# The outermost dimension of a transfer: loads and stores of the last rows of x and w1 with rows outermost, in place of 2 or 4 groups

## The chip, the cores and the metric

One core of one Trainium2 chip. The time is device microseconds of one execution of the whole program; lower is better. A profiled execution gives the trace from which the views below are taken.

## The reference

x has 2048 rows of 576 numbers. All is float32.

```python
xn = layernorm(x)
s  = linear_attention(xn, wqkv) @ wo          # 32 heads of 18, phi(t) = where(t>0, t+1, exp(t)) + 1e-6
h  = gelu(xn @ w1 + b1)                       # w1 [576, 4608]
g  = silu(h @ w2 + b2)                        # w2 [4608, 576]
out = x + s * g
```

The attention has no softmax over rows: per head it is (phi(q) (phi(k)^T v)) / (phi(q) z), with z the sum of phi(k) over the rows.

## The kernel before

**Precision.** Each matrix operand is kept as a high part (float32r) and the rest that the high part leaves out, and a product is high x high + high x rest + rest x high. ScalarE (ACT) makes the high part, VectorE (DVE) subtracts it to get the rest (`set_hi`, `set_lo`, L649 to L653).

**First stage.** For each of 16 tiles of 128 rows of x (loop at L431): load (`load_x`, three tiles ahead), layernorm on DVE with a power on GpSimd (POOL), transposes on TensorE (PE, tile `pt`), then the projections to k (`pk`) and v (`pv`) at L226 and the state phi(k)^T v. Beside it the loop prepares weights for later: it loads w2 (`w2_load`), makes sums of its blocks, splits them and stores them as operands (`w2_store`, L313); and it does the same for the last 64 rows of w1 (`we_load` L326, `we_sums` L331 on POOL, `we_hi`, `we_lo`, `we_store` L346). There are five groups q of the latter; each leaves a tile `w1h` of 128 rows with a high and a low part of 7 x 128 columns side by side, and `we_store` writes each part to `we_dram`.

**Second stage.** The same for q: project, normalize, transpose, and `attend` (`ps_s`, L626), which multiplies with kv already folded into wo and stores s to `s_dram`. Beside it the class `XSums` makes the sums of blocks of x that the main loop needs, and the class `Rest` (L758) does that for the last 64 of the 576 columns: `gather` and `whole` collect them, `split` makes high and low parts and writes them with four stores to `rq_dram` (L795).

**Main loop.** x @ w1 and h @ w2 are each done on 2 x 2 blocks with seven products in place of eight. The 2048 rows are two halves, and each half goes through nine chunks of four column tiles of w1: 18 steps. A step does 14 up products (`Up.step`, PE line L959, tiles `a`, `b`, `zy`, `e`; seven matmuls each) and then seven down products (`product`, PE line L1089, tile `pm`, 168 matmuls), added into `macc`. The 512 first rows of w1 come in through `W1` in the first half (raw, L679; the operands are made on chip and stored, L647) and through `W1Loaded` in the second half (L733, L740). The last 64 rows of w1 come through `load_we` (L662, DMA at L666), twice a step: a tile `we` of 128 partitions, in which partitions 0 to 63 and 64 to 127 hold the same 64 rows (32 rows of high part, 32 of low part). The seventh matmul of each product uses it against the matching tile of x, whose 128 rows are loaded by `load_rest` (L807): the high part twice and the low part twice, 32 rows each. In the second half a step also loads all seven operands of w2 (L1029), and for one tile of the first half's rows the finished sum, s and x (`finish_load`, L1178 to L1180, tiles `fin`); POOL combines them (`finish`, L1184, L1185) and stores the output (L1186). Between the halves seven tiles of x of 1 MB are loaded (`load_x_part`, L1252). The last step has no blocks to sum: it uses w2 as it is (`down_plain`, tile `pd`, L1209) and writes the last outputs.

**What sets the order.** PE, ACT, DVE and POOL follow an order written out in the code: each action of a step has a place (`add(base + n, ...)`, run by `at_step` after each product). All DMAs are issued by SyncE (SP) in one list, in order; an issue first waits for the tile or the DRAM tensor it touches, and for one of eight DMA semaphores, which are used in turn: so at most eight transfers are under way, and the issue after them waits until the one eight before it has landed.

The layouts around the change, each followed by the access it is used with:

```python
    rq_dram = dram.tile([2, 8, P, 512], F32, name="rq_dram")              # L117
    we_dram = dram.tile([4 * WG, 2, 32, WB * P], F32, name="we_dram")     # L118
        d = we_dram.rearrange("(g q) v r c -> q v g r c", q=WG)           # L344: store of 4 groups x 32 rows
            bass.AP(tensor=src.tensor, offset=src.offset, ap=[[0, 2], [WB * P, 64], [1, WB * P]]),  # L668
```

## Time and profile before

| | |
|---|---|
| time, median of 3 runs | 1250.49 us (1247.34 to 1253.26) |
| the profiled execution's own time | 1250.95 us |
| its span, first to last instruction | 1249.2 us |
| mean granted PE clock | 0.953 |
| DMA queue of SyncE | 85135 packets, 264.94 MB, 62.4% of 16 engines' span |
| HBM | 166.69 MB read, 96.27 MB written |

The span is cut into instructions per engine; "busy" is the union of their times. A window is a stretch of the span, with the busy time of each engine in it, the clock that PE was granted (1.00 is full), the mean busy share of the core's 16 DMA engines, and the rate in GB/s. A line of 40 digits cuts a window (or the span) in 40 slices; a digit is the busy share in tenths. The chain is followed back from the last instruction to what released each step; a row has its start, its length and what it was, "DMA a<-b" being a transfer from its issue to its landing, and "SPq" SyncE's own list. A row on waits says who waited for whom, the total, how often, and the longest. A row on issues has duration ns min/median/max of the issuing instruction and its first and last start.

### The profile page before, as it was taken

Reading aid. Unit: us, or ns where it says so; the run is one execution under the profiler, and the core shown is the slowest. Engines: PE = TensorE matmul, PEld = TensorE weight load, DVE = VectorE, ACT = ScalarE, POOL = GpSimd, SP = SyncE. Lnnn points to the kernel's source line nnn. Section 1 sums busy time; section 2 is a strip of 40 time slices with the busy share of each in tenths; the row PEclk is TensorE's granted clock in tenths of the full one; section 3 lists DMA queues with packets and bytes.
Section 4 is the critical chain, followed back from the end, with each engine's and each line's share of the span. In section 5 each row is a group of like instructions: output and inputs, shape, how many; then the busy total and the mean of one; then the engine's idle time right before and its main releaser. Section 6 shows DMA issues by size and latency. Waiting matters only on the chain.

```text
span 1249.2 us, 18534 instructions
## 1 busy us (share of the span) xinstructions
PE 1136.9 (91%) x6972; PEld 1044.1 (84%) x6972; DVE 816.6 (65%) x1159; ACT 456.7 (37%) x771; POOL 448.4 (36%) x392
## 2 busy tenths in 40 slices
PE   8965799999889899999999995989989989989888
PEld 8865798999779789989989984878787977978868
DVE  6733465989656778878877874547365563654657
ACT  4422353334342543544444352314123232232333
POOL 4634463433234534533553451304134042240430
PEclk9987899999989999999999997989989999999889
DMA  7655653256576495586567587876676566766542
GB/s 282 219 218 188 262 213 119 80 188 238 170 286 228 169 330 215 198 297 252 201 256 281 206 255 260 287 236 178 199 232 196 176 189 189 217 201 186 180 157 87
DMA packets 85224, 266.12 MB, mean 213 GB/s; under 512 B 8973, under 2 KB 19469, under 8 KB 81551
## 3 DMA queue, kind: packets, MB, share of 16 engines
q1 hardware_dynamic: 85135, 264.94, 62.4%
q8 instruction: 55, 0.90, 0.3%
q14 instruction: 34, 0.28, 0.1%
HBM read 166.69 MB, written 96.27 MB: 210 GB/s over the span
## 4 chain that ended last, share of the span: by engine, by line
PE 59%; DMA 27%; DVE 4%; SPq 3%; POOL 2%; issue 2%; ACT 1%; POOLq 0%; DVEq 0%; ACTq 0%
PE pm L1089 24%; PE e L959 6%; PE zy L959 6%; PE a L959 5%; DMA w1u<-w1e 3%; PE pv L226 3%; PE pq L226 3%; PE b L959 3%; DMA fin4h<-x 3%; PE pk L226 3%; PE ps_s L626 2%; DMA we<-op 2%; DMA we_dram<-w1h 2%; DMA fin2h<-x 2%; PE pd L1209 2%
## 5 line engine op out<-in xcount | busy, mean ns | idle before, releaser
L1096 DVE TENSOR_TENSOR macc<-pm,macc 128x576 f32<-128x576 f32 x218 | 164.4, 754 | 68.1 <-PE pm L1089 66.5
L650 ACT CAST h_h<-g 128x512 fp32r<-128x512 f32 x204 | 121.5, 620 | 174.0 <-PE pm L1089 138.2
L653 DVE TENSOR_TENSOR h_l<-g,h_h 128x512 fp32r<-128x512 f32 x204 | 168.1, 829 | 6.9 <-ACT h_h L650 6.6
L1184 POOL TENSOR_TENSOR fin1l<-fin1h,fin1l 128x288 f32<-128x288 f32 x8 | 6.5, 818 | 258.0 <-DMA fin1l<-s_dram 155.6
L1058 POOL TENSOR_TENSOR mid<-g 128x512 f32<-128x512 f32 x34 | 44.6, 1312 | 104.1 <-ACT g L967 104.1
L1052 POOL TENSOR_TENSOR g<-g 128x512 f32<-128x512 f32 x34 | 53.0, 1559 | 38.5 <-DVE h_l L653 36.6
L967 ACT ACTIVATE g<-b,b1c 128x512 f32<-128x512 f32 x36 | 24.8, 689 | 114.6 <-DVE b L985 114.6
L976 ACT COPY mid<-a 128x512 f32<-128x512 f32 x36 | 21.1, 587 | 123.8 <-PE a L959 123.8
L979 DVE TENSOR_TENSOR mid<-b,mid 128x512 f32<-128x512 f32 x36 | 24.7, 687 | 61.1 <-PE b L959 59.4
L694 POOL TENSOR_TENSOR w1raw<-w1raw 128x256 f32<-128x256 f32 x18 | 16.9, 937 | 130.6 <-DVE wa L710 130.6
L653 DVE TENSOR_TENSOR h_l<-mid,h_h 128x512 fp32r<-128x512 f32 x34 | 44.9, 1321 | 21.7 <-ACT h_h L650 21.0
L959 PE MATMUL a<-xh,wa 128*128 128x512 f32 x144 | 51.7, 399 | 6.9 <-ACT g L967 3.8
L1055 POOL TENSOR_TENSOR g<-g 128x512 f32<-128x512 f32 x34 | 54.5, 1604 | 2.7
L959 PE MATMUL a<-h0r,wa 128*128 128x512 f32 x144 | 50.6, 392 | 0.0
L982 DVE TENSOR_TENSOR mid<-zy,mid 128x512 f32<-128x512 f32 x36 | 24.9, 691 | 37.3 <-PE zy L959 37.2
L203 PE MATMUL pt<-ident,xn 128*128 128x128 f32 x80 | 13.5, 306 | 38.3 <-ACT xn L198 37.0
L1049 POOL TENSOR_TENSOR g<-g 128x512 f32<-128x512 f32 x34 | 46.4, 1364 | 2.7
L985 DVE TENSOR_TENSOR b<-e,mid 128x512 f32<-128x512 f32 x36 | 25.2, 699 | 31.7 <-PE e L959 31.6
L959 PE MATMUL b<-s2r,we 128*128 128x512 f32 x126 | 34.7, 418 | 12.0 <-issue 7.7
L591 POOL TENSOR_TENSOR pbuf<-phiq,den 128x576 f32<-128x576 f32 x16 | 20.0, 1251 | 66.7 <-DVE den L590 52.1
L203 PEld LDWEIGHTS pt<-ident,xn 128*128 128x128 f32 x80 | 10.2, 155 | 40.4 <-ACT xn L198 38.6
L295 POOL TENSOR_TENSOR w2r<-w2r 128x576 f32<-128x576 f32 x27 | 41.5, 1543 | 0.7
(810 smaller groups left out, 3700.0 us busy)
## 6 DMA issues: line engine op xcount, KB each, us to landing
we<-we_dram SPq DMA_DIRECT2D x36, 448.0 KB
op<-w2o SPq DMA_DIRECT2D x27, 576.0 KB
w2raw<-w SPq DMA_DIRECT2D x10, 1152.0 KB
w2r<-w SPq DMA_DIRECT2D x9, 1152.0 KB
w1raw<-w SPq DMA_DIRECT2D x18, 512.0 KB
op_a<-wa SPq DMA_DIRECT2D x18, 512.0 KB
op_c<-wc SPq DMA_DIRECT2D x18, 512.0 KB
op_d<-wd SPq DMA_DIRECT2D x18, 512.0 KB
```

Of the source, the lines that this page charges most:

```text
L226: nc.tensor.matmul(ps[:, h, :HD], st, w[:, k, h * HD : (h + 1) * HD], start=(i == 0), stop=(i == len(seq) - 1),)
L295: nc.gpsimd.tensor_tensor(dst, a, b, op=SUB)
L650: nc.scalar.copy(pair[0], src)
L653: eng.tensor_tensor(pair[1], src, pair[0].bitcast(F32), op=SUB)
L959: nc.tensor.matmul(ps, st, mv, start=first and n == 0, stop=n == len(seq) - 1, skip_group_check=True,)
L985: tt(B, E, u2_sb, op=ADD)
L1049: tt(src[5, pr], A(1, 0), A(1, 1), op=ADD)
L1052: tt(src[6, pr], src[5, pr], A(0, 0), op=SUB)
L1055: tt(src[3, pr], A(0, 1), src[6, pr], op=SUB)
L1058: tt(src[7, pr], A(0, 0), A(1, 0), op=SUB)
L1089: nc.tensor.matmul(ps[:, q, :HD], hs[p][st][:, cs], m[:, p, :], start=(n == 0 and i not in CHAIN), stop=(n == len(seq) - 1), skip_group_ch ...
L1096: nc.vector.tensor_tensor(dst, src, dst, op=ADD)
```

## The change

Three tensors or accesses take another shape. `rq_dram` and `we_dram` now hold the rows in DRAM in the order in which they stand on chip, row by row, with the high and the low part of a row side by side. A store therefore has the 128 partitions as its outermost dimension on both sides: one store per group in `we_store` (high and low part together, 896 KB) in place of two with four groups outermost; two stores in `Rest.split` in place of four. A load of `we` becomes two loads of 64 rows, one for each half of the partitions, in place of one load whose source has an outermost dimension of 2 with step 0. A load of a rest becomes two loads of 64 partitions, each with 32 source rows outermost and each row repeated twice inside.

```diff
-    rq_dram = dram.tile([2, 8, P, 512], F32, name="rq_dram")
-    we_dram = dram.tile([4 * WG, 2, 32, WB * P], F32, name="we_dram")
+    rq_dram = dram.tile([2, 2, P, 2, 512], F32, name="rq_dram")
+    we_dram = dram.tile([WG, P, 2, WB * P], F32, name="we_dram")
...
     def we_store(q):
-        d = we_dram.rearrange("(g q) v r c -> q v g r c", q=WG)
-        for v in range(2):
-            nc.sync.dma_start(d[q, v], we_op(q, v).bitcast(F32))
+        src = we["h", q % 2][:, : 2 * WB * P].bitcast(F32)
+        nc.sync.dma_start(we_dram[q].rearrange("p v c -> p (v c)"), src)
...
     def load_we(n):
 
         we_sb[n] = w1p.tile([P, WB, P], F32R, tag="we", name=f"we_{n}", bufs=2)
-        src = we_dram[n % NP]
-        nc.sync.dma_start(
-            we_sb[n].bitcast(F32).rearrange("p b c -> p (b c)"),
-            bass.AP(tensor=src.tensor, offset=src.offset, ap=[[0, 2], [WB * P, 64], [1, WB * P]]),
-        )
+        dst = we_sb[n].bitcast(F32).rearrange("p b c -> p (b c)")
+        g, q = divmod(n % NP, WG)
+        src = we_dram[q, 32 * g : 32 * g + 32].rearrange("r v c -> (r v) c")
+        for k in range(2):
+            nc.sync.dma_start(dst[64 * k : 64 * k + 64], src)
...
         def split(self, k):
             src = (self.q, self.e)[k]
-            h, l = self.two(f"s{k}")
+            h, l = t = self.two(f"s{k}")
             nc.scalar.copy(h, src)
             nc.vector.tensor_tensor(l, src, h.bitcast(F32), op=SUB)
-            for n, v in enumerate((h, h, l, l)):
-                nc.sync.dma_start(
-                    rq_dram[self.half, 4 * k : 4 * k + 4, 32 * n : 32 * n + 32], v.bitcast(F32)
-                )
+            for v in range(2):
+                nc.sync.dma_start(rq_dram[self.half, k, :, v], t[v].bitcast(F32))
...
     def load_rest(half, i, dst):
 
-        nc.sync.dma_start(dst.bitcast(F32), rq_dram[half, REST_AT[i]])
+        k, at = divmod(REST_AT[i], 4)
+        for v in range(2):
+            src = rq_dram[half, k, 32 * at : 32 * at + 32, v]
+            nc.sync.dma_start(
+                dst[64 * v : 64 * v + 64].bitcast(F32),
+                bass.AP(tensor=src.tensor, offset=src.offset, ap=[[1024, 32], [0, 2], [1, 512]]),
+            )
```

## The prediction

> **What bounds the kernel now.** I read the page first, then the chain of work that ended last, a table of windows by stage, and the windows in which TensorE (PE) waits.

> ```profile
> span 1249.2 us, 18534 instructions
> ...
> PE 1136.9 (91%) x6972; PEld 1044.1 (84%) x6972; DVE 816.6 (65%) x1159; ACT 456.7 (37%) x771; POOL 448.4 (36%) x392
> ...
> PE 59%; DMA 27%; DVE 4%; SPq 3%; POOL 2%; issue 2%; ACT 1%; POOLq 0%; DVEq 0%; ACTq 0%
> ```

> PE does nearly all the work, yet over a quarter of the chain is transfers. The windows show where (columns: busy us of each engine with its instructions, granted PE clock, busy share of the 16 DMA engines, GB/s):

> ```profile
> 32.67:140.05 107.38, 70.33 (x499) 68.75 (x498) 50.63 (x85) 34.73 (x57) 45.59 (x52) 0.83 0.61 219
> 140.05:194.50 54.45, 54.45 (x422) 54.45 (x423) 37.02 (x63) 25.13 (x42) 29.54 (x23) 0.99 0.59 220
> 202.00:336.30 134.30, 132.98 (x986) 128.58 (x985) 109.44 (x165) 51.80 (x96) 45.86 (x36) 1.00 0.47 151
> 336.30:445.60 109.30, 96.55 (x534) 85.45 (x533) 69.74 (x98) 42.74 (x74) 40.52 (x34) 0.94 0.65 235
> 445.60:760.60 315.00, 315.00 (x1864) 285.68 (x1863) 255.14 (x348) 143.13 (x250) 139.19 (x116) 1.00 0.69 245
> 760.60:880.50 119.90, 97.84 (x535) 85.66 (x534) 62.42 (x80) 33.90 (x52) 30.16 (x22) 0.89 0.75 245
> 880.50:1187.90 307.40, 283.48 (x1597) 256.11 (x1597) 170.36 (x228) 88.42 (x144) 87.80 (x72) 0.95 0.63 195
> 1187.90:1249.20 61.30, 50.05 (x292) 44.95 (x290) 39.16 (x50) 20.01 (x32) 12.10 (x7) 0.93 0.35 122
> ```

> From 336.30 on these are steps of the main loop: 0 and 1; 2 to 8; 9 and 10; 11 to 16; 17. Steps 2 to 8 take 315.00 / 7 = **45.0 us** each with PE busy throughout and its clock at 1.00: that is the floor of a step, and a PE that never rests isn't throttled here. The other steps lose time, and so does the first stage. There, the chain gives one row per value projection (pv) of a tile of x:

> ```profile
> 14.19 3.84 PE pv L226 x28
> ...
> 23.61 3.77 PE pv L226 x28
> ...
> 32.67 3.77 PE pv L226 x28
> ...
> 48.73 40.46 DMA w1u<-w1e x2
> 89.25 25.18 DMA we_dram<-w1h
> ...
> 140.05 4.44 PE pv L226 x28
> ...
> 194.50 3.77 PE pv L226 x28
> ...
> 329.56 14.05 DMA xh<-rq_dram
> ...
> 738.83 12.73 SPq L740
> ...
> 788.07 1.61 PE a L959 x7
> ...
> 804.76 27.71 DMA we<-op
> ...
> 928.85 18.28 DMA fin4h<-x
> ...
> 1198.36 2.27 DMA fin3l<-s_dram
> ...
> 1218.25 22.42 PE pd L1209 x168
> ```

> Of sixteen tiles the rows at 14.19, 23.61 and 32.67 are the first three and 194.50 is the last. At the pace of the undisturbed rows (9.1 us) 140.05 is the tenth: the last six tiles took (194.50 - 140.05) / 6 = 9.08 us each. The seven tiles between 32.67 and 140.05 should take 63.5 us and took 107.4: **43.9 us lost**, and the chain there is a load of w1e and a store to we_dram. Note also that small transfers with nothing ahead of them land in 2.27 us, others after 14 to 28 us.

> Why so late? One step (13, 984.0 to 1035.4) in 40 slices of 1.285 us, and a wait of the first stage:

> ```profile
> DMA  9997311259857920301689999999811111697999
> GB/s 259 322 254 207 113 50 53 72 154 262 309 161 164 373 98 26 121 0 56 136 328 379 402 393 268 263 257 257 243 67 50 49 50 51 144 350 249 267 277 271
> ```

> ```profile
> 95.00:101.00 6.00, 0.00 (x0) 0.00 (x0) 0.00 (x0) 0.00 (x0) 0.00 (x0) 0.50 0.24 84
> ```

> A row of ones at 50 GB/s is two engines of sixteen (2/16 = 0.125), 25 GB/s each; 0.24 is four of sixteen. Everything on PE is idle at 95 to 101, and four engines still carry data. The program has two kinds of transfer with such a count outermost: the load of we (outermost dimension the two repeats) and the stores to we_dram and rq_dram (outermost dimension 4).

> ```profile
> we<-we_dram SPq DMA_DIRECT2D x36, 448.0 KB
> we_dram<-w1h SPq DMA_DIRECT2D x10, 448.0 KB
> rq_dram<-wa_rest0s SPq DMA_DIRECT2D x8, 256.0 KB
> ```

> So **two (or four) engines are the bound, not all sixteen.** Step 13 moves 195 GB/s x 51.4 us = 10.0 MB. Without its two loads of we (0.92 MB) an engine has 9.1/16 = 0.57 MB; at the rate of a busy engine there (195 / 0.63 / 16 = 19.3 GB/s) 29.5 us. The two engines have 2 x 448 KB / 2 / 25 GB/s = 18.3 us more: 47.8 us, above the 45.0 of PE. All later transfers have a share on those two engines and land behind it.

> **The change, part by part.** (1) The load of we becomes two loads of 64 rows; an engine gets 1/16 of both: 2.3 us a step in place of 18.3 on two. (2) Ten stores of 448 KB on four engines (10 x 448 KB / 4 / 25 GB/s = 46 us on each of the four) become five of 896 KB over 128 rows, 11.5 us on each engine. (3) Sixteen stores to rq_dram become eight over 128 rows. They lie in 202.00:336.30, where PE is busy 132.98 of 134.30 us: nothing to gain. (4) Fourteen loads of rests become 28 of 64 rows, with 32 outermost in the source. The order of instructions on PE, DVE, ACT and POOL is the same in both programs; only SyncE's list changes, by 36 + 14 - 5 - 8 = 37 more issues.

> ```profile
> L666 SPq DMA_DIRECT2D we<-we_dram x36: 499/511/4835, 329.0 to 1167.4; - x36
> ...
> L809 SPq DMA_DIRECT2D rx<-rq_dram x8: 319/323/432, 326.7 to 778.7; - x8
> ```

> ```profile
> SPq L1029 <- PE pm L1089: 171.5, 40, 12.4
> ...
> SPq L1179 <- DMA we<-we_dram: 35.2, 5, 8.8
> ```

> An issue holds SyncE 0.32 to 0.51 us: 37 x 0.5 = 19 us in all, one us a step, beside 171.5 us in which that queue waits for PE products. I cost it at nothing; without that cover it is 19 us. What stands behind an extra issue is the next load of weights, due half a step later. The second row shows another cost that goes: each transfer takes one of eight semaphores in turn, so an issue waits until the one eight before it has landed, and a load of final tiles (L1179) waits on a load of we that it has nothing to do with.

> What the stages gain, with engines evenly loaded:
> - *First stage.* Lost 43.9. The DMA work of the window is 0.61 x 107.38 = 65.5 us of all engines, against 63.5 us of PE: it just fits, some is pushed into 140.05:194.50 (0.59 busy), and x is loaded three tiles ahead. I leave 9 and take **35**. Lower end: no window above packs better than 0.75, which makes 87 us: gain 20.
> - *Steps 0 and 1.* Lost 109.30 - 90 = 19.3. A load of we at 329 holds the rests behind it for 14.05 us, and PE waits 6.3 us for it (row below). I take **17** (6 to 19).
> - *Steps 9 and 10.* Lost 29.9. Work 0.75 x 119.9 = 90 us against 90 of PE: tight, since the seven 1 MB tiles of x for the second half come here, but the stores and later weights in it aren't urgent. I take **21**; if 0.75 is all that packs, nothing.
> - *Steps 11 to 16.* Lost 307.40 - 270 = 37.4. Work 0.63 x 307.4 = 194 us over 270: 0.72, barely above the 0.69 at which steps 2 to 8 lose nothing. What is late now is the final tiles (chain: 18.28 us for 144 KB), which hold POOL and then PE; their tiles are asked for at a step's start and used some 10 us into it, and 2 to 8 us will do. I take **34**; at 0.69 the stage takes 281 us: gain 26.
> - *Step 17.* Fourteen products of 1.61 us (row at 788.07) should put its down product at 1210.4; it starts at 1218.25. Of 7.8 I take **6** (0 to 7.8).

> ```profile
> PEld a L959 <- DMA we<-we_dram: 6.3, 1, 6.3
> ```

> Sum: 35 + 17 + 21 + 34 + 6 = **113 us**. The profiled execution took 1250.95 us (span 1249.2 and 1.75 around it; the median of the runs is 1250.49), so 1250.95 - 113 = **1138 us**. Lower ends: 20 + 6 + 0 + 26 + 0 = 52, 1199 us. All losses gone: 138.3, 1112 us.

> [...]

> **Rivals.**
> - *Packing.* The work is spread but doesn't pack better than it does now, because SyncE is one queue in order and waits for PE and DVE (171.5 us above). For: no stage is over 0.75 busy. Against: step 13 has ten slices at 9 between its holes. It gives the lower ends: **1199**.
> - *The spread fails.* If the rows are dealt to engines by another rule than the outermost count, we stays on few engines: **1251**. Against: loads and stores of 128 rows reach 300 to 400 GB/s in step 13, which two engines can't.
> - *Slower: eight transfers in flight.* A step of the second half issues 25 transfers (7 of w2, 8 of w1, 2 of we, 6 final loads, 2 outputs), then 27. Eight at a time over 307.40 / 6 = 51.2 us allow 8 x 51.2 / 25 = 16.4 us to each. If landing stayed that slow, for HBM's sake and not for the two engines, a step would take 27 x 16.4 / 8 = 55.3 us: 4.1 more in steps 10 to 16, 29 us, **1280**. It decides from a mean landing above 8 x 45 / 27 = 13.3 us. Against: 2.27 us with nothing ahead, and fourteen idle engines while others wait.

> **How the numbers follow.** Forecast 0.70 (its own range 1112 to 1165), packing 0.18 (1165 to 1199), no spread 0.05, eight in flight 0.07. The range 1112 to 1199 takes in the first two and all bounds. A measurement of this kernel tells about 0.5% from no change: faster 0.88, same 0.05, slower 0.07.

> **What would show it.** Steps 11 to 16 at 45 to 46 us with PE's clock at 1.00; the tiles between pv rows 3 and 10 at 9 to 10.5 us; no row of ones in a step's slices; landings in the chain under 10 us; the same bytes as in the row below at a higher mean rate.

> ```profile
> DMA packets 85224, 266.12 MB, mean 213 GB/s; under 512 B 8973, under 2 KB 19469, under 8 KB 81551
> ```

> I am wrong if rows of ones stay, if steps stay near 50 us with even slices (packing, or eight in flight), or if the first stage stays above 85 us.

## The result and the profile after

| | before | changed |
|---|---|---|
| time, median | 1248.91 us (1247.11 to 1253.26, 4 runs) | 1123.46 us (1120.33 to 1125.7, 4 runs) |
| ratio | | 0.8989, 95% interval 0.8954 to 0.9025 |
| profiled execution / span | 1250.95 / 1249.2 us | 1125.7 / 1124.0 us |
| mean granted PE clock | 0.953 | 0.996 |

The changed kernel is faster by 10%. Its page, in the lines that answer to those of before:

```profile
span 1124.0 us, 18604 instructions
...
PE 1104.1 (98%) x6972; PEld 1019.6 (91%) x6972; DVE 815.1 (73%) x1159; ACT 455.9 (41%) x771; POOL 449.5 (40%) x392
...
DMA packets 84969, 264.03 MB, mean 235 GB/s; under 512 B 10381, under 2 KB 20877, under 8 KB 81295
...
q1 hardware_dynamic: 84879, 262.85, 68.8%
...
PE 90%; DMA 5%; DVE 2%; issue 1%; SPq 0%; ACT 0%; POOL 0%; DVEq 0%; ACTq 0%; POOLq 0%
```

PE is busy 98% of the span. Its busy time itself fell by 33 us, and the granted clock shows why: every stage in the table of before in which PE rested more than 2 us had a clock of 0.95 or less, and steps 11 to 16, the same work, were busy for 283.48 us at 0.95 before and for 270.00 us at 1.00 now. Transfers make 5% of the chain in place of 27%. The windows by stage, cut at the same places of the program (columns as in the table of before):

```profile
32.11:154.70 122.59, 118.22 (x919) 117.11 (x919) 89.91 (x147) 60.02 (x98) 73.75 (x75) 1.00 0.77 290
154.70:295.50 140.80, 140.29 (x1043) 136.13 (x1043) 113.02 (x169) 53.76 (x99) 48.14 (x43) 1.00 0.45 153
295.50:385.70 90.20, 90.13 (x534) 81.49 (x533) 72.30 (x98) 42.78 (x74) 40.92 (x34) 1.00 0.77 271
385.70:700.70 315.00, 315.00 (x1864) 285.69 (x1863) 255.17 (x349) 143.14 (x250) 139.18 (x116) 1.00 0.74 255
700.70:799.60 98.90, 93.46 (x534) 83.32 (x533) 60.27 (x80) 33.73 (x52) 29.94 (x22) 0.97 0.84 281
799.60:1069.60 270.00, 270.00 (x1598) 244.88 (x1597) 169.60 (x228) 87.55 (x144) 90.10 (x73) 1.00 0.71 216
1069.60:1124.00 54.40, 48.56 (x292) 43.77 (x290) 35.09 (x50) 20.00 (x32) 11.49 (x7) 0.98 0.38 131
```

Steps 2 to 8 (385.70) are unchanged at 45.0 us. Steps 11 to 16 (799.60 on) take 270.00 / 6 = 45.0 us, with PE busy for all of it: exactly the floor. The first of these windows, cut at the tenth pv row:

```profile
32.11:100.92 68.81, 64.44 (x498) 63.33 (x498) 51.86 (x83) 33.85 (x55) 44.85 (x52) 1.00 0.87 322
100.92:154.70 53.78, 53.78 (x423) 53.78 (x422) 38.05 (x65) 26.18 (x44) 28.90 (x23) 1.00 0.65 249
```

PE still rests for 4.4 us in the first seven tiles, and not at all in the last six. Where the time came from, stage by stage:

| stage | before | after | gained | forecast |
|---|---|---|---|---|
| pv row 3 to pv row 16 | 161.8 | 122.6 | 39.2 | 35 |
| second stage, to the main loop | 141.8 | 140.8 | 1.0 | 0 |
| steps 0 and 1 | 109.3 | 90.2 | 19.1 | 17 |
| steps 9 and 10 | 119.9 | 98.9 | 21.0 | 21 |
| steps 11 to 16 | 307.4 | 270.0 | 37.4 | 34 |
| step 17 to the end | 61.3 | 54.4 | 6.9 | 6 |

With 0.6 us ahead of pv row 3 that is 125.2 us, the difference of the spans. The slices of step 13 (889.6 to 934.6, 1.125 us each) show what changed:

```profile
DMA  8986400578899999978878899787649259197565
GB/s 277 221 352 231 138 0 0 157 182 302 259 226 257 267 198 188 179 169 315 215 266 299 281 320 203 212 270 205 229 152 352 78 139 352 51 256 273 158 217 140
```

There is no run of ones any more. In the slices of zeros all the engines rest together. Few waits are left on PE. The first rows of the view of who waited for whom, on PE:

```profile
PE pt L203 <- ACT xn L198: 4.4, 4, 1.1
PE e L962 <- DMA rx<-rq_dram: 3.6, 1, 3.6
...
PE e L962 <- DMA s1r<-x_dram: 1.0, 1, 1.0
PE zy L962 <- DMA l1r<-x_dram: 0.9, 1, 0.9
```

The last three are all in step 9, the one step of the loop that is still late: 53.9 us, of the 98.90 in the row at 700.70. The second half of the experiments is about it.

### The profile page after: what moved, and what is told of

It is laid out like the page before. It is cut to its first block, busy times and chain, and to the rows that moved or that the text cites. A ratio compares the mean times of both kernels' runs of the same rounds, so it can differ in the third digit from the quotient of the medians.

```text
span 1124.0 us, 18604 instructions
## 1 busy us (share of the span) xinstructions
PE 1104.1 (98%) x6972; PEld 1019.6 (91%) x6972; DVE 815.1 (73%) x1159; ACT 455.9 (41%) x771; POOL 449.5 (40%) x392
## 2 busy tenths in 40 slices
DMA packets 84969, 264.03 MB, mean 235 GB/s; under 512 B 10381, under 2 KB 20877, under 8 KB 81295
## 3 DMA queue, kind: packets, MB, share of 16 engines
q1 hardware_dynamic: 84879, 262.85, 68.8%
## 4 chain that ended last, share of the span: by engine, by line
PE 90%; DMA 5%; DVE 2%; issue 1%; SPq 0%; ACT 0%; POOL 0%; DVEq 0%; ACTq 0%; POOLq 0%
PE pm L1092 32%; PE a L962 10%; PE e L962 10%; PE zy L962 10%; PE pq L226 5%; PE b L962 5%; PE ps_s L625 5%; PE pv L226 4%; PE pk L226 4%; PE pd L1212 2%; DMA rx<-rq_dram 1%; DMA w1u<-w1e 1%; PE ps_kva L263 1%; DMA we<-we_dram 1%; DMA w__7651<-op 1%
## 5 line engine op out<-in xcount | busy, mean ns | idle before, releaser
L652 DVE TENSOR_TENSOR h_l<-g,h_h 128x512 fp32r<-128x512 f32 x204 | 164.8, 815 | 0.0
L1061 POOL TENSOR_TENSOR mid<-g 128x512 f32<-128x512 f32 x34 | 43.9, 1292 | 134.3 <-ACT g L970 134.3
L1055 POOL TENSOR_TENSOR g<-g 128x512 f32<-128x512 f32 x34 | 55.1, 1620 | 57.7 <-DVE h_l L652 56.4
L1058 POOL TENSOR_TENSOR g<-g 128x512 f32<-128x512 f32 x34 | 55.4, 1630 | 2.7
L1052 POOL TENSOR_TENSOR g<-g 128x512 f32<-128x512 f32 x34 | 46.7, 1373 | 2.7
L995 DVE TENSOR_TENSOR e<-e,mid 128x512 f32<-128x512 f32 x36 | 24.9, 691 | 22.8 <-PE e L962 22.7
L970 ACT ACTIVATE g<-e,b1c 128x512 f32<-128x512 f32 x36 | 24.9, 691 | 34.0 <-DVE e L995 33.9
L226 PE MATMUL pv<-wv_h,xh 128*128 128x288 f32 x160 | 35.5, 304 | 0.0
```

Source lines behind the costliest of these rows:

```text
L226: nc.tensor.matmul(ps[:, h, :HD], st, w[:, k, h * HD : (h + 1) * HD], start=(i == 0), stop=(i == len(seq) - 1),)
L652: eng.tensor_tensor(pair[1], src, pair[0].bitcast(F32), op=SUB)
L970: nc.scalar.activation(g, ps, AF.Gelu_apprx_tanh, bias=b1c[:, f : f + 1])
L1052: tt(src[5, pr], A(1, 0), A(1, 1), op=ADD)
L1055: tt(src[6, pr], src[5, pr], A(0, 0), op=SUB)
L1058: tt(src[3, pr], A(0, 1), src[6, pr], op=SUB)
```

## The experiments

**Which part, and which side.** Theory: the time came from the loads of we on two engines and the stores to we_dram on four. Rivals: the rests matter; the layout (rows side by side in DRAM) is what helps; both sides are needed together.

*e1_we_only*: the rests as before, in cost. (The row order within them follows the new we, so that the products stay the same.)

```diff
-            for v in range(2):
-                nc.sync.dma_start(rq_dram[self.half, k, :, v], t[v].bitcast(F32))
+            d = rq_dram[self.half].rearrange("i (k r t) c -> i k t r c", k=2, t=2)
+            for n, v in enumerate((h, h, l, l)):
+                nc.sync.dma_start(d[4 * k : 4 * k + 4, n // 2, n % 2], v.bitcast(F32))
...
+        nc.sync.dma_start(dst.bitcast(F32), rq_dram[half, REST_AT[i]])
```

> The we part alone is changed; the rests are stored in sixteen stores with 4 outermost and loaded with 128 rows, as before. Theory of few engines (the time came from the loads of we on two engines and the stores of we on four): 1123 to 1130 us, since the stores of the rests lie where PE is busy all the time. Rival, the rests matter (their two-part loads let steps 0 and 9 start): 1135 us or more.

Measured 1118.44 us (ratio to before 0.8961, 0.8925 to 0.8997): all of the gain, and less time than the 1123 to 1130 us expected. It is also 5 us under the whole change, but the two ran on different chips and their intervals overlap. What the traces do show is step 9: 45.0 us here, 53.9 in the changed kernel.

*e2_rest_only*: stores and loads of we as before.

```diff
-    we_dram = dram.tile([WG, P, 2, WB * P], F32, name="we_dram")
+    we_dram = dram.tile([4 * WG, 32, 2, WB * P], F32, name="we_dram")
...
+        d = we_dram.rearrange("(g q) r v c -> q v g r c", q=WG)
+        for v in range(2):
+            nc.sync.dma_start(d[q, v], we_op(q, v).bitcast(F32))
...
+        src = we_dram[n % NP]
+        nc.sync.dma_start(
+            we_sb[n].bitcast(F32).rearrange("p b c -> p (b c)"),
+            bass.AP(tensor=src.tensor, offset=src.offset, ap=[[0, 2], [WB * P, 64], [1, WB * P]]),
+        )
```

> The rests alone are changed; we is stored with 4 groups outermost and loaded with 2 repeats outermost, as before. Few engines: 1243 to 1252 us, nothing gained. Rival, the rests matter: below 1240 us.

Measured 1246.07 us (0.9971, 0.9949 to 0.9993): next to nothing, so the rests aren't the cause of the gain. By stages it is a trade: steps 9 and 10 take 130.7 us in place of 119.9, and the others give that back.

*e3_undo_load*: the changed kernel, with only the load of we back in one transfer.

```diff
-        src = we_dram[q, 32 * g : 32 * g + 32].rearrange("r v c -> (r v) c")
-        for k in range(2):
-            nc.sync.dma_start(dst[64 * k : 64 * k + 64], src)
+        src = we_dram[q, 32 * g : 32 * g + 32]
+        nc.sync.dma_start(
+            we_sb[n].bitcast(F32).rearrange("p b c -> p (b c)"),
+            bass.AP(tensor=src.tensor, offset=src.offset, ap=[[0, 2], [WB * P, 64], [1, WB * P]]),
+        )
```

> The changed kernel with the load of we alone put back to one transfer with 2 repeats outermost; the DRAM layout, the stores and the bytes are those of the changed kernel. Few engines: the first stage keeps its gain of 39 us and the main loop goes back, 1249 - 39 = 1210 us, steps 11 to 16 near 51 us, rows of ones in their slices. Rival, locality (rows side by side in DRAM are what helps): 1123 to 1130 us.

Measured 1207.92 us (0.966, 0.9632 to 0.9688). The main loop starts at 297.6 us (295.5 in the changed kernel, 336.3 before), and its steps are slow again, much as before (steps 11 to 16 at 49.5 us each, against 51.2): windows of the first stage and of steps 11 to 16 with this kernel, and its slices of step 13 (939.9 to 993.2):

```profile
32.00:154.00 122.00, 117.56 (x916) 116.46 (x916) 87.44 (x144) 59.80 (x98) 75.23 (x78) 1.00 0.77 288
846.90:1143.60 296.70, 279.75 (x1599) 252.83 (x1598) 169.23 (x228) 88.43 (x144) 88.31 (x72) 0.97 0.64 195
```

```profile
DMA  9999721145876860300889999999511113899999
GB/s 264 274 301 241 217 92 52 50 148 101 349 231 151 282 250 27 123 2 5 173 338 338 418 384 319 265 272 245 139 48 51 49 51 73 252 409 355 254 267 248
```

The ones at 50 GB/s are back with one access pattern over the same bytes at the same addresses. Locality falls.

*e4_undo_store*: the changed kernel, with only the store of we back in ten transfers with 4 groups outermost (layout and store as in e2_rest_only, the load in two parts).

> The changed kernel with the stores of we alone put back to ten stores with 4 groups outermost. Few engines: the first stage loses its 39 us again and the main loop keeps its gain, 1123 + 39 = 1162 us. Rival, locality: 1123 to 1130 us. Rival, both parts needed together (landings share the same eight semaphores all through): above 1180 us.

Measured 1160.47 us (0.9283, 0.925 to 0.9316). Its chain of work in the first stage is that of the kernel before, and its steps 11 to 16 take 45.0 us:

```profile
32.59 3.77 PE pv L226 x28
...
48.67 39.26 DMA w1u<-w1e x2
87.99 24.91 DMA we_dram<-w1h
...
114.79 16.76 DMA x<-x
...
138.99 3.76 PE pv L226 x28
```

The two sides add up. Undoing the load costs 1207.92 - 1123.46 = 84.5 us, undoing the store 37.0; together 121.5, and the kernel with both undone (e2_rest_only) is 122.6 above the changed one. They are two separate bounds in two separate stages.

**Is it the number of engines?** The load was also split in two, so the split or the shorter transfer could be what helps. A gap in DRAM after every 16, 8 or 4 rows keeps the outermost dimension of each 64-row load at 2, 4 or 8 groups while all else stands.

```diff
+    RP = 16                                   # 8, 4 in the next two
-    we_dram = dram.tile([WG, P, 2, WB * P], F32, name="we_dram")
+    we_dram = dram.tile([WG, P // RP, RP * 2 * WB * P + 512], F32, name="we_dram")
...
+        d = we_dram[q, :, : RP * 2 * WB * P].rearrange("a (r c) -> a r c", r=RP)
+        nc.sync.dma_start(d, src)
...
+        na = 32 // RP
+        src = we_dram[q, na * g : na * g + na, : RP * 2 * WB * P]
+        src = src.rearrange("a (r c) -> a r c", c=WB * P)
```

> The changed kernel with a gap of 2 KB in we_dram after every 16 rows of a group, so that each of the two loads of 64 rows has 2 groups of 32 rows outermost (and the store 8 groups of 16). Two issues, two engines. Few engines: like the kernel with one load over 2 repeats, 1205 to 1220 us. Rival, the split in two issues is what helps: 1123 to 1130 us.

> The gap stands after every 8 rows: each load has 4 groups outermost. Few engines as a bound (a step is lost only when the busiest engines need more than the 45 us of PE): 29.5 + 9.2 = 38.7 us in a step, so steps 11 to 16 at 45 us and 1123 to 1135 us. Rival, in proportion (each us on the busiest engine delays something): of the 84 us that go from 18.3 us a step to 2.3 us, those from 9.2 us to 2.3 us, 36 us: 1160 us.

> The gap stands after every 4 rows: each load has 8 groups outermost, 4.6 us a step on eight engines. As a bound: 1121 to 1127 us. In proportion: 1135 us.

| groups outermost | time, us | ratio to before (interval) | step 0 | step 9 | steps 11 to 16, mean |
|---|---|---|---|---|---|
| 2 (e5) | 1218.76 | 0.9757 (0.973 to 0.9783) | 58.2 | 70.2 | 49.9 |
| 4 (e6) | 1142.62 | 0.9157 (0.9134 to 0.918) | 50.5 | 59.7 | 45.0 |
| 8 (e7) | 1129.71 | 0.9048 (0.9025 to 0.9071) | 45.6 | 59.5 | 45.0 |
| 64 rows (changed) | 1123.46 | 0.8989 (0.8954 to 0.9025) | 45.3 | 53.9 | 45.0 |

Two issues on two engines are as slow as one: it isn't the split. (It is 10.8 us above e3_undo_load, on another chip. Half of that stands ahead of the main loop, which starts at 302.9 us in place of 297.6; its store has 8 groups outermost. The other half is not explained.) With four groups, the windows of step 0, of steps 1 to 8, of step 9 and of steps 11 to 16:

```profile
295.80:346.20 50.40, 46.70 (x267) 41.81 (x267) 35.77 (x48) 22.44 (x38) 20.48 (x17) 0.97 0.77 274
346.20:706.20 360.00, 360.00 (x2130) 326.49 (x2129) 291.90 (x398) 163.50 (x286) 159.75 (x133) 1.00 0.70 248
706.20:765.90 59.70, 48.90 (x268) 42.23 (x267) 31.99 (x42) 19.16 (x28) 15.07 (x10) 0.89 0.90 283
812.00:1082.00 270.00, 270.00 (x1599) 244.86 (x1598) 169.56 (x228) 87.54 (x144) 89.64 (x73) 1.00 0.70 217
```

With four groups the six steps that lost 37 us before lose nothing: by the estimate, half the load on each of twice the engines, 38.7 us of work on the busiest engines fits in 45. So in the steady steps the busy engines are a bound with a threshold, and "in proportion" falls there. Both runs miss what was expected, 1142.6 against 1123 to 1135 and 1129.7 against 1121 to 1127. Most of it lies in steps 0 and 9: with four groups they take 11.0 of the 12.4 us by which the span is longer than that of the changed kernel (1136.4 against 1124.0), and with eight groups step 9 takes 5.6 of 7.0 (1131.0). Step 9 isn't in proportion either, since it is as long with eight groups as with four (59.5 and 59.7); these runs don't show what sets it.

**Why step 9 is still late.** The changed kernel loses 8.9 us there and e1_we_only none. The row of its chain in which PE waits, and three windows behind the wait:

```profile
697.76 15.21 DMA rx<-rq_dram
```

```profile
713.00:714.00 1.00, 0.89 (x2) 0.82 (x3) 0.08 (x1) 0.00 (x0) 0.00 (x0) 0.50 0.31 96
714.00:719.00 5.00, 5.00 (x13) 3.83 (x13) 0.62 (x1) 1.38 (x2) 0.00 (x0) 0.53 0.98 356
720.00:730.00 10.00, 10.00 (x46) 8.19 (x45) 4.72 (x8) 4.81 (x9) 3.73 (x3) 1.00 1.03 349
```

PE rests for 5.4 us, and the last and longest of its waits is for a rest. Behind it the matmuls have half the clock (0.50 and 0.53) for some 6 us, which makes the other 3.5 us. Two theories of why the loads are late: loads to 64 neighbouring partitions are slower in themselves (the median packet of 3584 bytes, those of we, took 199 ns in the trace of the changed kernel and 144 ns in that of the kernel before), or their number fills the eight places for transfers under way. *e8_one_we* has one load of we over 128 partitions, and puts the two parts of a rest on every second partition:

```diff
-        for k in range(2):
-            nc.sync.dma_start(dst[64 * k : 64 * k + 64], src)
+        nc.sync.dma_start(
+            we_sb[n].bitcast(F32).rearrange("p b c -> p (b c)"),
+            bass.AP(tensor=src.tensor, offset=src.offset, ap=[[WB * P, 64], [0, 2], [1, WB * P]]),
+        )
...
-                dst[64 * v : 64 * v + 64].bitcast(F32),
+                dst[v : v + 127 : 2].bitcast(F32),
```

> The changed kernel with the load of we as one transfer of 128 partitions (64 rows outermost, each repeated inside), and the two loads of a rest go to every second partition in place of the lower and the upper half. Few engines: spread over sixteen as before, 36 issues fewer; 1115 to 1125 us. [...] Rival, the number of issues sets the loss of step 9 (eight in flight): it falls to 5 to 7 us.

Measured 1116.26 us (0.8944, 0.8925 to 0.8963), step 9 at 45.0 us: no loss at all, but it changed both things at once. *e9_pairs_apart* keeps the number of issues and changes only the partitions:

```diff
-            nc.sync.dma_start(dst[64 * k : 64 * k + 64], src)
+            nc.sync.dma_start(dst[k : k + 127 : 2], src)
...
-                dst[64 * v : 64 * v + 64].bitcast(F32),
+                dst[v : v + 127 : 2].bitcast(F32),
```

> As many issues as the changed kernel, all on sixteen engines; but both loads of a pair (we and rests) go to every second partition in place of the lower and the upper half. [...] Rival, the number of issues (eight in flight): step 9 stays at 53 to 54 us, 1121 to 1126 us.

> The kernel with one load of we over 128 partitions once more, beside the changed kernel on the same chip: 1115 to 1119 us, 0.5% under the changed kernel by either theory of step 9.

> The changed kernel once more on the same chip: 1121 to 1126 us, step 9 at 53 to 54 us.

Measured beside each other: e9_pairs_apart 1116.68 us (0.8953, 0.8922 to 0.8984), e10_one_we_again 1116.55 us (0.8953, 0.8922 to 0.8985), e11_after_again 1123.26 us (0.9004, 0.8973 to 0.9036; its step 9 took 51.2 us, less than expected). Step 9 in the changed kernel:

```profile
700.70:754.60 53.90, 48.46 (x268) 42.51 (x267) 32.01 (x42) 19.16 (x28) 15.07 (x10) 0.94 0.97 329
```

again in e11_after_again, with its line on the DMA queue:

```profile
700.90:752.10 51.20, 47.07 (x268) 41.77 (x267) 31.92 (x42) 19.16 (x28) 15.07 (x10) 0.97 1.00 344
```

```profile
q1 hardware_dynamic: 84879, 262.85, 69.2%
```

and the same two of e9_pairs_apart:

```profile
700.70:745.70 45.00, 45.00 (x268) 40.81 (x267) 31.80 (x42) 19.05 (x28) 14.95 (x10) 1.00 0.95 352
```

```profile
q1 hardware_dynamic: 84879, 262.85, 66.6%
```

All are as good as full in step 9 (0.97, 1.00, 0.95), but e9_pairs_apart moves 352 GB/s in place of 329 and 344. And on the same chip the same 84879 packets with the same 262.85 MB take 66.6% of a span of 1115.0 us, 742.6 us of sixteen engines, against 69.2% of 1121.5, 776.1: **33.5 us less with only the partitions changed**. In the traces the median packet of 3584 bytes (the loads of we) took 208 ns in e11_after_again and 140 ns in e9_pairs_apart. To halves of the partitions it took 145 ns with two and with four groups outermost (e5_pair_2, e6_pair_4) and 176 ns with eight (e7_pair_8). The number of issues falls as a theory: 36 more of them (e9 against e10) change nothing, 1116.68 to 1116.55, and with 28 loads of rests both have step 9 at 46 us or less.

By an estimate the loads that these 33.5 us belong to, 36 x 448 KB and 28 x 128 KB, take 56 us of all the engines at 359 GB/s (219 GB/s at a busy share of 0.61, the row at 32.67 in the table of before). By that, loads in halves cost some six tenths on top.

Which halves cost step 9 its time? The loads of we alone don't. In e1_we_only they are in halves too, their packets take 204 ns in the middle, and the queue is busy for longer than in the changed kernel (70.1% of 1114.9 us, 781.5 us); only the rests come in over all partitions, and step 9 takes 45.0 us. Where the rests are in halves and the load of we is one transfer on two engines, in e2_rest_only and e3_undo_load, steps 9 and 10 take 130.7 and 131.3 us, against 119.9 before. So the loss goes with the rests in two halves, part (4) of the change. A kernel with only the rests in halves and all else well spread was not run, so how much the halves of we add is open.

## Why the prediction was right, point by point

- *The bound.* Right, and shown from both sides: the main loop is lost again by e3_undo_load and e5_pair_2, the first stage by e4_undo_store. The estimate of 47.8 us on two engines, against steps of 51.2 us, lies above the 45.0 of PE as it should, and 38.7 us in e6_pair_4 lies below; where between the two the threshold is was not measured.
- *The sum.* 113 forecast, 125.2 measured. Every stage gained its term or more. The largest difference is in the first stage: 9 us kept back, 4.8 needed (122.59 against thirteen tiles of 9.06). That a tight DMA would still cost PE something was right: PE rests for 4.4 us in the first seven tiles. Some 3 us of DMA work moved into the later tiles, as forecast (0.65 x 53.78 = 35.0 us, against 0.59 x 54.45 = 32.1). In steps 11 to 16 the 3.4 us kept back weren't needed at all.
- *The rests' stores.* Forecast at no gain; the second stage moved by 1.0 us.
- *37 more issues at nothing.* Right: e9 against e10 has 36 of them, and no difference.
- *Loads to one half of the partitions.* The sum has no term for them. They cost 1123.26 - 1116.68 = 6.6 us, of which step 9 has 6.2 (51.2 to 45.0) and step 10 nothing. The pairs of we alone cost e1_we_only nothing in step 9. The loss goes with the rests in halves, whose 14 extra loads the sum put at nothing.
- *The rival of packing* fell: steps 9 and 10 pack to 0.84, step 9 alone to 0.97, the first seven tiles to 0.87. Shares of 0.6 to 0.75 were low because fourteen engines had to wait for two (50 GB/s in the rows of ones).
- *Eight in flight* fell: a step with 27 issues runs at the floor. *The spread fails*: no, the rows of ones are gone. That each engine gets a sixteenth of the new loads and stores was the author's assumption: no view of the runs shows it engine by engine. What they show is slices without a row of ones and a busy share of up to 0.97 (step 9).
- *The signs to look for.* The tiles between pv rows 3 and 10 take 9.05 to 10.4 us, as forecast. Landings in the chain are under 10 us but for one, the 15.21 us of a rest in step 9.
- *Wrong in a sign to look for:* "the same bytes". They fell from 266.12 to 264.03 MB. The rests are stored once in place of twice, eight stores of 256 KB fewer, 2.1 MB; the number of stores was counted, their bytes weren't.

## What to carry to other kernels

A mean busy share of the DMA engines of 0.61 to 0.65 (the rows of the first stage and of steps 0, 1 and 11 to 16 before) didn't mean here that they had room: look at the slices for runs of a constant low digit (ones at 50 GB/s were two engines of sixteen, a share of 0.24 was four), and at small transfers that land late (18.28 us for 144 KB before). Then look for transfers whose outermost dimension is small, such as a load with a repeat of step 0 (84.5 us here) or a store of four groups (37.0 us), and put the rows outermost with the repeat inside. Don't trade it for transfers to one half of the partitions: parts on every second partition, with the load of we in two parts or in one over all 128, took this kernel from 1123.3 to 1116.7 and 1116.6 us.
